# Swapping the first two weight loads of a decode kernel on one Trainium2 core

## The chip, the cores and the metric

The kernel runs on one core of one Trainium2 chip. The metric is device time in microseconds (us), the median of several executions; lower is better. In the profiles PE is the matrix engine (TensorE) and PEld its weight loads, DVE the vector, ACT the scalar and POOL the GpSimd engine; SP only issues transfers here. Profiles show one execution; their clock starts at the beginning of its span, and the span is about 1.3 us shorter than the device time.

## The reference, cut to what matters

One token passes through grouped-query attention with a long cache (part A) and through an MLP (part B), and the two results are added.

```python
x  = A_x                                    # [1, 1, 1024]
xn = layernorm(x)
# A: q = layernorm'd x @ wq; softmax over 4 KV heads x 65536 positions; @ wo
# B, called with x = xn:
h  = gelu(layernorm(x) @ w1)
g0 = pad(h[:, :, 0*c:1*c], one row in front)[:, :S]     # S = 1: only the padding is left
...                                                     # g1, g2, g3 likewise
hs = concat([g0, g1, g2, g3]) @ w2
x1 = x + hs
h2 = gelu(layernorm(x1) @ w3) @ w4
return x + A(xn) + (x1 + h2)
```

All data is bfloat16. What must be read is 169.87 MB: 134 MB of K and V, and the rest weights. wq and wo have 64 KB in each of 128 partitions (8.39 MB), w3 and w4 56 KB, w1 and w2 16 KB (2.1 MB).

## The kernel before

Three 64 KB slots per partition (`KV[:, 0..2]`) hold everything that is loaded. SP's queue carries all loads but one; x goes out on ACT's queue. These are the opening loads:

```python
_dma(q_act, chan("x"), lambda e: e.dma_start(out=x_bf, in_=...), writes=[b_x])   # 2 KB
kv_load(0, "s0", rows_src(A_wq, 0, 8), 8 * HQD)               # slot 0: wq, 64 KB a partition
kv_load(1, "w1", rows_src(B_w1, 0, 8), 8 * D, b_w1)           # slot 1, front: w1, 16 KB
_dma(q_sp, chan("w2"), ... KV[:, 1, 8 * D:16 * D] ...)        # slot 1, behind: w2, 16 KB
kv_load(2, "s2", rows_src(B_w3, 0, 8), 8 * F)                 # slot 2: w3, 56 KB
```

The compute of the opening follows in program order. Each `issue` sends a K or V block of 8.39 MB once its slot is free:

```python
cast x; constants; layer_norm(x)     # needs x
q projection                         # needs wq (slot 0) and the layer norm
issue(3)                             # first K block into slot 0
q to its layout; second layer norm
proj(w1); gelu; proj(w2)             # w2 times zeros
issue(4)                             # first V block into slot 1
third layer norm; proj(w3); gelu
issue(5)                             # second K block into slot 2
# then 8 blocks: transpose K, QK, exp, PV; each ends by issuing the next V and K
```

At the end of the program's construction, the first instruction of SP and of ACT, which must be a DMA, is moved in front of the barrier that opens the program:

```python
for eng in (nc.sync.engine, nc.scalar.engine):
    first = next(i for i in code[n_before:] if i.engine == eng)
    ...
    code.insert(code.index(heads[eng]), first)
```

Of the kernel before, what the change touches and what calls it, by code (L numbers as in the profile page):

```python
# [99 lines left out]
def _deps(q, reads, writes):  # L100
    evs = [e for b in reads for e in b.w.items()]
    for b in writes:
        evs += list(b.w.items()) + list(b.r.items())
    q.wait_all(evs, in_order=q.name == "pe")


def _done(ev, reads, writes, partial=False):
    for b in reads:
        b.add_read(ev)
    for b in writes:  # L110
        if partial:
            b.add_write(ev)
        else:
            b.set_write(ev)
# [24 lines left out]
def _dma(q, chan, fn, reads=(), writes=(), partial=False):  # L139
    _deps(q, reads, writes)  # L140
    chan.n += 1
    ev = q.dma(fn, chan.sem, 16 * chan.n)
    _done(ev, reads, writes, partial)
    return ev


def bass_parallel_sum__gqa_block_cached__mixer_s_mlp__decode_kernel(
# [16 lines left out]
    HQD = A_wq.shape[1]  # L164
# [14 lines left out]
    with ExitStack() as es:  # L179
# [8 lines left out]
        def sem(name):  # L188
            return E(nc.semaphore(name))
# [84 lines left out]
        def chan(name):  # L274
            if name not in chans:
                chans[name] = _DmaChan(sem("d_" + name))
            return chans[name]
# [11 lines left out]
        def kv_load(s, ch, src, n, bufs=None):  # L289
            _dma(q_sp, chan(ch), lambda e: e.dma_start(out=KV[:, s, 0:n], in_=src), writes=b_KV[s] if bufs is None else bufs)  # L290

        def rows_src(w, r0, nrow):
            return w.rearrange("(p r) n -> p (r n)", p=P)[:, r0 * w.shape[1]:(r0 + nrow) * w.shape[1]]

        _dma(q_act, chan("x"), lambda e: e.dma_start(out=x_bf, in_=A_x[0, 0, :].rearrange("(p j) -> p j", p=P)), writes=[b_x])
        kv_load(0, "s0", rows_src(A_wq, 0, 8), 8 * HQD)
        b_w1 = b_KV[1][0:2]
        b_w2 = b_KV[1][2:4]
        kv_load(1, "w1", rows_src(B_w1, 0, 8), 8 * D, b_w1)
        _dma(q_sp, chan("w2"), lambda e: e.dma_start(out=KV[:, 1, 8 * D:16 * D], in_=rows_src(B_w2, 0, 8)), writes=b_w2)  # L300
        kv_load(2, "s2", rows_src(B_w3, 0, 8), 8 * F)

# [427 lines left out]
```

## Time and profile before

| | before |
|---|---|
| time, median of the first 3 runs | 400.29 us |
| span of the profiled run | 399.3 us |
| load queue's packets, share of 16 DMA engines' span | 98.7% |
| DVE / PE busy | 55% / 45% |
| x lands, q projection starts | 22.4 us, 27.66 us |
| first K / first V / second K issued | 34.2 / 52.3 / 71.5 us |

From the page of the kernel before: the busy times (busy us, share of the span, instructions), the DMA queues (packets, MB, share), and the chain that ended last, by engine.

```profile
span 399.3 us, 3500 instructions
...
PE 177.8 (45%) x1539; PEld 61.1 (15%) x1539; DVE 221.3 (55%) x260; ACT 23.9 (6%) x50; POOL 7.7 (2%) x31
...
q1 hardware_dynamic: 3608, 169.87, 98.7%
...
q10 hardware_dynamic: 144, 0.00, 0.0%
...
DMA 58%; DVE 25%; PE 14%; issue 1%; ACT 1%; SPq 1%; POOL 0%
```

q1 is SP's queue with all the loads, and q10 is ACT's, with x alone. No compute engine is busy for more than 55% of the span, while q1's packets fill 98.7% of what 16 engines can do. The chain says 25% DVE, but that does not make DVE the limit: while DVE transposes, the load queue is still full.

The timeline of the kernel before (start us, duration, engine, line, operation, output and input, and in brackets the idle time before it and what ended it):

```profile
0.00 0.39 SPq L290 DMA_DIRECT2D KV<-in_A_wq_dram  x1
0.12 0.37 ACTq L295 DMA_DIRECT2D KV<-in_A_x_dram  x1
...
22.38 0.17 DVE L339 CAST KV<-KV 128x8 f32<-128x8 bf16 x1 [22.38 <-DMA KV<-in_A_x_dram]
...
27.66 6.49 PE L379 MATMUL S_ps<-KV 128*32 128x512 bf16 x64 [1.36 <-DVE KV L359]
28.07 0.16 PEld L379 LDWEIGHTS S_ps<-KV 128*32 128x32 bf16 x4 [0.27 <-issue]
28.49 0.16 PEld L379 LDWEIGHTS S_ps<-KV 128*32 128x32 bf16 x4 [0.27 <-issue]
...
34.21 0.33 SPq L290 DMA_DIRECT2D KV<-in_A_k_cache_dram  x1
...
101.21 0.33 SPq L290 DMA_DIRECT2D KV<-in_A_v_cache_dram  x1
```

x is 2 KB and lands after 22 us. All of the opening's compute stands behind it: the q projection waits for the layer norm (its releaser is DVE), not for wq.

The end of the chain of waits (start us, us, what):

```profile
363.85 32.93 DMA KV<-in_B_w_dram
396.78 0.04 issue
```

The run ends 2.5 us after the last piece of w4 lands.

### The profile page before, as it was taken

Reading aid. Unit: us, or ns where it says so; the run is one execution under the profiler, and the core shown is the slowest. Engines: PE = TensorE matmul, PEld = TensorE weight load, DVE = VectorE, ACT = ScalarE, POOL = GpSimd, SP = SyncE. Lnnn points to the kernel's source line nnn. Section 1 sums busy time; section 2 is a strip of 40 time slices with the busy share of each in tenths; the row PEclk is TensorE's granted clock in tenths of the full one; section 3 lists DMA queues with packets and bytes.
Section 4 is the critical chain, followed back from the end, with each engine's and each line's share of the span. In section 5 each row is a group of like instructions: output and inputs, shape, how many; then the busy total and the mean of one; then the engine's idle time right before and its main releaser. Section 6 shows DMA issues by size and latency. Waiting matters only on the chain.

```text
span 399.3 us, 3500 instructions
## 1 busy us (share of the span) xinstructions
PE 177.8 (45%) x1539; PEld 61.1 (15%) x1539; DVE 221.3 (55%) x260; ACT 23.9 (6%) x50; POOL 7.7 (2%) x31
## 2 busy tenths in 40 slices
PE   0035669147134713560358036413661462147394
PEld 0022435012001110110012001100120110012232
DVE  0024230995298539843984597269647952895201
ACT  1000000011001100110011002000100110011000
POOL 5000000000000000000000000000000000000000
PEclk9998656555755665585557555855565558555979
DMA  9999899999999999999999999999999999999995
GB/s 420 420 387 487 382 441 479 440 415 427 415 427 427 433 474 433 420 427 420 433 427 433 473 433 420 421 420 433 433 433 473 433 420 420 420 433 433 416 424 219
DMA packets 3759, 169.97 MB, mean 426 GB/s; under 512 B 548, under 2 KB 552, under 8 KB 808
## 3 DMA queue, kind: packets, MB, share of 16 engines
q1 hardware_dynamic: 3608, 169.87, 98.7%
q8 instruction: 5, 0.08, 0.1%
q10 hardware_dynamic: 144, 0.00, 0.0%
q14 instruction: 2, 0.02, 0.0%
HBM read 169.87 MB, written 0.00 MB: 425 GB/s over the span
## 4 chain that ended last, share of the span: by engine, by line
DMA 58%; DVE 25%; PE 14%; issue 1%; ACT 1%; SPq 1%; POOL 0%
DMA KV<-in_A_k_cache_dram 44%; DVE KV L460 17%; DMA KV<-in_B_w_dram 8%; DMA KV<-in_A_x_dram 6%; PE S_ps L411 3%; PE OT_ps L518 3%; DVE mrow L481 2%; PE M_ps L426 2%; PE S_ps L474 2%; PE S_ps L379 2%; ACT p_sb L496 1%; DVE Yall L395 1%; PE PT_ps L505 1%; DVE pT_f L509 1%; DVE pT_f L419 1%
## 5 line engine op out<-in xcount | busy, mean ns | idle before, releaser
L460 DVE STREAM_TRANSPOSE KV<-KV 128x4096 f32<-128x4096 f32 x32 | 140.3, 4421 | 42.2 <-DMA KV<-in_A_k_cache_dram 42.2
L474 PE MATMUL S_ps<-KV,Ycur 128*32 128x512 bf16 x512 | 60.7, 623 | 126.1 <-DVE KV L460 126.1
L518 PE MATMUL OT_ps<-KV,pT_f 128*32 128x512 bf16 x512 | 46.6, 504 | 1.2 <-DVE pT_f L509 1.2
L474 PEld LDWEIGHTS S_ps<-KV,Ycur 128*32 128x32 bf16 x512 | 14.3, 126 | 158.1 <-DVE KV L460 140.5
L496 ACT ACTIVATE p_sb<-S_ps,brun 128x1024 bf16<-128x1024 f32 x16 | 17.8, 1114 | 274.7 <-DVE brun L494 174.3
L509 DVE STREAM_TRANSPOSE pT_f<-PT_ps 128x512 f32<-128x512 f32 x32 | 22.4, 701 | 14.0 <-PE PT_ps L505 14.0
L481 DVE TENSOR_REDUCE mrow<-S_ps 128x1 f32<-128x1024 f32 x16 | 19.3, 1204 | 11.3 <-PE S_ps L474 11.3
L484 PE MATMUL M_ps<-Rm,Lmat 128*128 128x16 bf16 x16 | 3.1, 194 | 38.0 <-DVE Rm L482 38.0
L505 PE MATMUL PT_ps<-p_sb,permR 128*128 128x512 bf16 x32 | 18.3, 573 | 0.8
L529 DVE SCALAR_TENSOR_TENSOR O_acc<-O_acc,ff,OT_ps 128x512 f32<-128x512 f32 x12 | 9.0, 747 | 14.4 <-PE OT_ps L518 14.4
L518 PEld LDWEIGHTS OT_ps<-KV,pT_f 128*32 128x32 bf16 x512 | 12.9, 114 | 23.6 <-issue 15.5
L411 PE MATMUL S_ps<-KV 128*32 128x512 bf16 x88 | 12.5, 571 | 2.7 <-DVE KV L359 2.7
L339 DVE CAST KV<-KV 128x8 f32<-128x8 bf16 x1 | 0.2, 172 | 22.4 <-DMA KV<-in_A_x_dram 22.4
L578 PE MATMUL S_ps<-KV,o_bf 128*1 128x512 bf16 x64 | 9.7, 476 | 4.8 <-DMA KV<-in_A_wo_dram 4.8
L484 PEld LDWEIGHTS M_ps<-Rm,Lmat 128*128 128x128 bf16 x16 | 1.7, 104 | 49.3 <-DVE Rm L482 49.3
L426 PE MATMUL M_ps<-ident_f,pT_f 64*128 64x2 f32 (+2 forms) x32 | 7.9, 372 | 2.4 <-DVE pT_f L419 2.4
L582 DVE COPY pT_f<-S_ps 1x512 f32<-1x512 f32 x1 | 0.7, 679 | 14.4 <-PE S_ps L578 14.4
L426 PEld LDWEIGHTS M_ps<-ident_f,pT_f 64*128 64x128 f32 (+2 forms) x32 | 7.7, 326 | 4.7 <-DVE pT_f L419 3.4
L419 DVE COPY pT_f<-S_ps 64x512 f32<-64x512 f32 (+1 forms) x3 | 2.1, 685 | 11.3 <-PE S_ps L411 11.3
L505 PEld LDWEIGHTS PT_ps<-p_sb,permR 128*128 128x128 bf16 x32 | 3.3, 102 | 27.2 <-ACT p_sb L496 14.7
L364 PE MATMUL M_ps<-KV 8*128 8x8 bf16 x1 | 0.2, 182 | 16.2 <-DVE Dmat_f L363 16.2
L379 PE MATMUL S_ps<-KV 128*32 128x512 bf16 x64 | 6.5, 593 | 1.4 <-DVE KV L359 1.4
(88 smaller groups left out, 88.8 us busy)
## 6 DMA issues: line engine op xcount, KB each, us to landing
KV<-in_B_w_dram SPq DMA_DIRECT2D x1, 7168.0 KB, 48.4
KV<-in_B_w_dram SPq DMA_DIRECT2D x1, 4352.0 KB, 27.4
KV<-in_B_w_dram SPq DMA_DIRECT2D x2, 2048.0 KB, 28.4
KV<-in_B_w_dram SPq DMA_DIRECT2D x1, 1792.0 KB, 31.4
KV<-in_B_w_dram SPq DMA_DIRECT2D x1, 768.0 KB, 32.8
KV<-in_B_w_dram SPq DMA_DIRECT2D x1, 256.0 KB, 32.9
KV<-in_A_k_cache_dram SPq DMA_DIRECT2D x8, 46.5
KV<-in_A_v_cache_dram SPq DMA_DIRECT2D x8, 28.0
```

The source lines that it names most:

```text
L379: fns.append(lambda e, j=j, b=b, jj=jj: e.matmul(S_ps[32 * jj:32 * jj + 32, b, :], xn_bf[:, j:j + 1].broadcast_to([P, 32]), KV[:, 0, j * H ...
L411: fns.append(lambda e, j=j, k=k, mv=mv: e.matmul(S_ps[32 * (k % 4):32 * (k % 4) + 32, bank + k // 4, :], vec[:, j:j + 1].broadcast_to([P, ...
L426: fns.append(lambda e, b=b, nb=nb, c=c: e.matmul(M_ps[:, c0 + 16 * b + c:c0 + 16 * b + 4 * nb:4], pT_f[0:32 * nb, b, c:512:4], ident_f[0:3 ...
L460: _op(q_dve, lambda e: e.transpose(out=KV32[:, s, o:o + 4096], in_=KV32[:, s, o:o + 4096]), reads=[b_KV[s][sub]], writes=[b_KV[s][sub]], l ...
L474: fns.append(lambda e, we=we, cm=cm, mv=mv: e.matmul(S_ps[32 * cm:32 * cm + 32, n % 4, :], Ycur[:, we, :, :].rearrange("p a g -> p (a g)") ...
L481: _op(q_dve, lambda e: e.reduce_max(mrow[:, k:k + 1], S_ps[:, 2 * k:2 * k + 2, :].rearrange("p b c -> p (b c)"), axis=AX.X), reads=b_S[2 * ...
L496: _op(q_act, lambda e: e.activation(p_sb[:, :, :].rearrange("p b c -> p (b c)"), S_ps[:, 2 * k:2 * k + 2, :].rearrange("p b c -> p (b c)") ...
L505: _op(q_pe, lambda e: e.matmul(PT_ps[:, :], permR[:, :], p_sb[:, n % 2, :], start=True, stop=True), reads=[b_p[n % 2], b_const], writes=[b ...
L509: _op(q_dve, lambda e: e.transpose(out=pT_f[:, n % 2, :], in_=PT_ps[:, :]), reads=[b_PT], writes=[b_pT[n % 2]], loop=True)
L518: fns.append(lambda e, q=q, q4=q4: e.matmul(OT_ps[32 * q4:32 * q4 + 32, g % 2, :], pT_bf[:, n % 2, q, :, 1], KV[:, s, 8192 * sub + 512 * q ...
L529: _op(q_dve, lambda e: e.scalar_tensor_tensor(out=O_acc[:, 0:512], in0=O_acc[:, 0:512], scalar=ff[:, k:k + 1], in1=OT_ps[:, k, :], op0=ALU ...
L578: _grp(q_pe, [lambda e, j=j, jj=jj: e.matmul(S_ps[32 * jj:32 * jj + 1, 1, :], o_bf[:, j:j + 1], KV[:, 0, j * D + 512 * jj:j * D + 512 * (j ...
```

## The change

Its intent: x and w1 should be there early, so that the opening's compute starts sooner, since the first load in front of the barrier is then short.

```diff
         _dma(q_act, chan("x"), ...)
-        kv_load(0, "s0", rows_src(A_wq, 0, 8), 8 * HQD)
         b_w1 = b_KV[1][0:2]
         b_w2 = b_KV[1][2:4]
         kv_load(1, "w1", rows_src(B_w1, 0, 8), 8 * D, b_w1)
+        kv_load(0, "s0", rows_src(A_wq, 0, 8), 8 * HQD)
         _dma(q_sp, chan("w2"), ...)
```

The instructions of every engine other than SP are the same, in the same order.

## The prediction

> **What bounds the kernel now.** DMA. The page's queue table gives the load queue 98.7% of the 16 engines' span, 169.87 MB at 425 GB/s; DVE is busy 55%, PE 45%. In the chain of waits DMA has 58%, and the last w4 part lands at 396.8 us of 399.3. So the time is a start of about 1.3 us, 169.87 MB at the stream's rate, and a tail of 2.5 us. It changes only if the bytes, the rate, or the filling of the load queue change.
>
> **What the change does.** Bytes and number of loads stay. wq (8.39 MB) and w1 (2.1 MB) swap places; all others keep theirs. The load before the barrier goes out at 0.0 us, the next at 0.91; w1 alone is 5.0 us of stream at 420 GB/s (windows of the first 20 us), so the queue doesn't run dry.
>
> The visible effect is on x (2 KB, ACT's queue). Before, x was issued at 0.12 and landed at 22.4 us, together with wq. Its queue has 144 packets, nine for each of 16 engines. The Trainium skill, "DMA: Bandwidth & Descriptors", section "Queues, rings and completion order", says that each engine takes packets in turn from the queue rows that have work. Then x's eight small packets per engine alternate with eight 64 KB rows of wq, and x ends when wq does; the trace agrees (22.2 us to landing for both). With 16 KB rows of w1 in front, x ends with w1: about 5.0 + 2.2 = 7.2 us, or one or two wq rows (2.5 us each: 64 KB at a sixteenth of 420 GB/s) later: 7 to 12 us.
>
> The work hanging on x (cast, constants, first layer norm) took 22.4 to 27.6 us in the timeline, 5.3 us on the chain. It now runs under wq's load and ends by 13 to 17 us. But wq lands 5.0 us later, at about 27.2. So the q projection starts at about 27.3 instead of 27.66: 5.3 gained, 5.0 given back. An early w1 gains nothing: its projection stands behind the q projection and the second layer norm in program order.
>
> **On the critical path.** Almost nothing. About 0.4 us earlier from the q projection on: first K issue 33.9 (34.2), first V 52.0 (52.3), second K 71.2 (71.5). These are early already: w3 lands at 50.4 us, so the first K is issued 16 us before the queue would empty; estimated at 430 GB/s, the first K lands near 70 and the first V near 90, so the other two lead by about 18 us each. Later pairs are issued 7 us or more ahead of the stream's end (101.2 against 108.6). The queue stays full with or without the 0.4 us, and the last weight still lands at 396.8.
>
> **Predicted: 400.2 us, range 399.4 to 401.0.** Chances: faster by over 2% 0.01, within 2% 0.98, slower by over 2% 0.01.
>
> **What would show each step right or wrong.** Waits: DVE's 22.4 us wait for x falls to 7 to 12; the q projection's first matmul waits for wq's DMA. Timeline: q projection at 27.0 to 27.6, first K issue at 33.5 to 34.2. Queue table: share 98.5 to 99%, same bytes. Chain: its beginning changes from x to wq, its end doesn't; last weight at 396.8 within 0.6.
>
> **What would make it wrong.** If x landed behind wq after all (27 us), the q projection would start at 32.5 and the second V would be issued near 106, still 2 us ahead of the stream: the same time. A different rate of the stream, or a bubble between the first two loads, could cost or give about a microsecond; 2% would need 8 us of empty queue, for which I see no place.

## More of the kernel before

With one token (S = 1) all four shifted groups are zero, so `hs` is zero for finite weights. The kernel uses this in part: it multiplies w2 by a vector of zeros.

## The result, and the profile after

The kernel with the change took 400.73 us (median of 6 runs, 400.67 to 400.83) against 400.46 us before (6 runs, 400.26 to 400.55). The ratio is 1.0008, with a 95% interval of 0.9995 to 1.0021: the same. A ratio here compares the runs of both kernels by their means, so it is not quite the ratio of the medians. Executions over 1.5% slower than the fastest of the same kernel are left out of the means.

The same parts of the page after the change:

```profile
span 399.5 us, 3484 instructions
...
PE 170.0 (43%) x1523; PEld 61.4 (15%) x1539; DVE 221.4 (55%) x260; ACT 23.9 (6%) x50; POOL 7.6 (2%) x31
...
q1 hardware_dynamic: 3608, 169.87, 98.6%
...
DMA 60%; DVE 24%; PE 13%; issue 1%; ACT 1%; SPq 1%; POOL 0%
```

(The 16 matmuls fewer are records missing from the trace: the weight loads are all there, and the profile of the repeat below has all 1539 matmuls and 177.3 us.) The timeline after the change:

```profile
0.00 0.39 SPq L290 DMA_DIRECT2D KV<-in_B_w_dram  x1
0.12 0.37 ACTq L295 DMA_DIRECT2D KV<-in_A_x_dram  x1
...
0.92 0.33 SPq L290 DMA_DIRECT2D KV<-in_A_wq_dram  x1
...
10.36 0.17 DVE L339 CAST KV<-KV 128x8 f32<-128x8 bf16 x1 [10.36 <-DMA KV<-in_A_x_dram]
...
15.41 0.17 DVE L359 CAST KV<-KV 128x8 bf16<-128x8 f32 x1
27.41 5.04 PE L379 MATMUL S_ps<-KV 128*32 128x512 bf16 x64 [13.13 <-DMA KV<-in_A_wq_dram]
...
32.49 0.33 SPq L290 DMA_DIRECT2D KV<-in_A_k_cache_dram  x1
```

x lands 12.0 us sooner and the layer norm is done at 15.6 us, also 12.0 us sooner. Then PE idles until wq lands at 27.3 us. The projection starts 0.25 us sooner than before, and its releaser is now wq's DMA. The end of the chain of waits:

```profile
364.05 32.91 DMA KV<-in_B_w_dram
396.96 0.04 issue
```

The last piece of w4 lands at 396.96 us (396.78 before). The 1.7 us that the first K block was issued sooner (32.49 against 34.21) are gone by then. The chain shows where such a lead goes. The second K block, in the kernel before and then after the change:

```profile
71.52 37.07 DMA KV<-in_A_k_cache_dram
```

```profile
69.42 38.91 DMA KV<-in_A_k_cache_dram
```

It was issued 2.1 us sooner and landed only 0.26 us sooner (108.33 against 108.59); the rest it spent queued behind earlier loads. The chain counts a load from its issue, so it runs back through the opening (x's DMA before, wq's after), although the runs below show that the opening has slack.

**Why x landed when it did.** The trace has a record of every DMA packet: its queue, size, start and duration. The next table is worked out from these records. It gives the starts, in us after the first load packet, of x's 144 packets, sorted and cut into nine sets of 16 (one for each engine's share: eight of 16 bytes, then the one that signals the end).

```
set       before          after
1         3.07 -  3.87    1.99 - 2.68
2         5.49 -  6.29    2.77 - 3.29
3         7.91 -  8.71    3.38 - 3.99
4        10.33 - 11.13    4.04 - 4.60
...
8        20.01 - 20.27    6.05 - 6.55
9        20.28 - 20.82    8.26 - 8.97
```

Before, the first eight sets are 2.42 us apart, which is the duration of one 64 KB packet (median of all 2304 in the trace, 128 of them wq's: 2.421 us). After, the first seven are 0.58 to 0.78 us apart, about the duration of a 16 KB packet (median of the 256 of w1 and w2: 0.611 us); the last set falls behind a 64 KB packet of wq and takes 2.2 us more. This is what the Trainium skill, "DMA: Bandwidth & Descriptors", section "Queues, rings and completion order", states: an engine with work in two queue rows takes whole packets from them in turn. Here the load of tiny packets on the second queue moved at the pace of the other queue's packets, one a turn.

### The profile page after: what moved, and what is told of

It reads as the page before. It is cut to its first block, busy times and chain, and to the rows that moved or that the text cites. A ratio compares the mean times of both kernels' runs of the same rounds, so it can differ in the third digit from the quotient of the medians.

```text
span 399.5 us, 3484 instructions
## 1 busy us (share of the span) xinstructions
PE 170.0 (43%) x1523; PEld 61.4 (15%) x1539; DVE 221.4 (55%) x260; ACT 23.9 (6%) x50; POOL 7.6 (2%) x31
## 3 DMA queue, kind: packets, MB, share of 16 engines
q1 hardware_dynamic: 3608, 169.87, 98.6%
HBM read 169.87 MB, written 0.00 MB: 425 GB/s over the span
## 4 chain that ended last, share of the span: by engine, by line
DMA 60%; DVE 24%; PE 13%; issue 1%; ACT 1%; SPq 1%; POOL 0%
DMA KV<-in_A_k_cache_dram 45%; DVE KV L460 17%; DMA KV<-in_B_w_dram 8%; DMA KV<-in_A_wq_dram 7%; PE S_ps L411 3%; PE OT_ps L518 3%; DVE mrow L481 2%; PE M_ps L426 2%; PE S_ps L474 2%; PE S_ps L379 1%; ACT p_sb L496 1%; DVE Yall L395 1%; DVE pT_f L509 1%; DVE pT_f L419 1%; PE PT_ps L505 0%
## 5 line engine op out<-in xcount | busy, mean ns | idle before, releaser
L518 PE MATMUL OT_ps<-KV,pT_f 128*32 128x512 bf16 x512 | 47.6, 516 | 3.9 <-issue 3.1
L509 DVE STREAM_TRANSPOSE pT_f<-PT_ps 128x512 f32<-128x512 f32 x32 | 22.4, 701 | 14.0 <-PE PT_ps L505 14.0
L411 PE MATMUL S_ps<-KV 128*32 128x512 bf16 x88 | 12.2, 539 | 2.7 <-DVE KV L359 2.7
L379 PE MATMUL S_ps<-KV 128*32 128x512 bf16 x64 | 5.0, 484 | 13.1 <-DMA KV<-in_A_wq_dram 13.1
L505 PE MATMUL PT_ps<-p_sb,permR 128*128 128x512 bf16 x16 | 9.7, 608 | 0.8
```

Source lines behind the costliest of these rows:

```text
L379: fns.append(lambda e, j=j, b=b, jj=jj: e.matmul(S_ps[32 * jj:32 * jj + 32, b, :], xn_bf[:, j:j + 1].broadcast_to([P, 32]), KV[:, 0, j * H ...
L411: fns.append(lambda e, j=j, k=k, mv=mv: e.matmul(S_ps[32 * (k % 4):32 * (k % 4) + 32, bank + k // 4, :], vec[:, j:j + 1].broadcast_to([P, ...
L505: _op(q_pe, lambda e: e.matmul(PT_ps[:, :], permR[:, :], p_sb[:, n % 2, :], start=True, stop=True), reads=[b_p[n % 2], b_const], writes=[b ...
L509: _op(q_dve, lambda e: e.transpose(out=pT_f[:, n % 2, :], in_=PT_ps[:, :]), reads=[b_PT], writes=[b_pT[n % 2]], loop=True)
L518: fns.append(lambda e, q=q, q4=q4: e.matmul(OT_ps[32 * q4:32 * q4 + 32, g % 2, :], pT_bf[:, n % 2, q, :, 1], KV[:, s, 8192 * sub + 512 * q ...
```

## The experiments

All runs gave correct results. The kernel before ran beside them: 400.53 us (9 runs) beside the first four, 400.47 us (7 runs) beside the last two.

Two theories were set against each other. The *stream theory* is the prediction's: 169.87 MB must pass the 16 DMA engines, the load queue never runs empty, and the opening's compute only has to be early enough to keep it so. The *rival* says that the opening's chain is on the critical path, and that the change gained nothing only because wq, now 5 us later, gave back what x had gained.

### The change again

No edit to the changed kernel.

> The change again, with five rounds, to see whether its 0.2 to 0.3 us over the kernel before is real. The packet records of the two traces show the 16 DMA engines idle for 0.38 us on average in the first 20 us of the stream with the change and 0.18 us before. If that start is the cause: 0.1 to 0.3 us slower again (400.6 to 400.8 against 400.4), with the last weight again 0.2 us later. If it is chance: 0.0 within 0.1 us.

It took 400.6 us (5 runs) against 400.53: ratio 1.0003 (0.9989 to 1.0017). The engines' idle time in the first 20 us of the stream was 0.21 us this time (0.18 before, 0.38 in the first profile of the change), and the last weight landed at 396.77 us. So the difference of 0.27 us between the first two medians is not a property of the change that these runs can show.

### x in front of wq on the same queue

```diff
-        _dma(q_act, chan("x"), ...)
+        _dma(q_sp, chan("x"), ...)
         kv_load(0, "s0", rows_src(A_wq, 0, 8), 8 * HQD)
 ...
-        for eng in (nc.sync.engine, nc.scalar.engine):
+        for eng in (nc.sync.engine, nc.sync.engine):
```

> x and then wq on the same queue, both in front of the opening barrier. x lands at 2 to 4 us, wq at 22.5 to 23; the first layer norm runs under wq, and nothing is given back by a later wq. Theory (the DMA stream bounds the kernel, the opening only moves slack): the q projection starts near 22.8 us, 5 us sooner than in both kernels, and the time stays 400.0 to 401.0. Rival (the opening chain is on the critical path, and the change gained nothing only because the later wq gave the 5 us back): 395 to 396 us.

It took 400.85 us (5 runs), ratio 1.0009 (0.9995 to 1.0022): the same. Its timeline:

```profile
1.65 1.15 DVE L339 CAST KV<-KV 128x8 f32<-128x8 bf16 x1 [1.65 <-DMA KV<-in_A_x_dram]
22.54 5.38 PE L379 MATMUL S_ps<-KV 128*32 128x512 bf16 x64 [11.39 <-DMA KV<-in_A_wq_dram]
...
27.96 0.33 SPq L290 DMA_DIRECT2D KV<-in_A_k_cache_dram  x1
46.48 0.33 SPq L290 DMA_DIRECT2D KV<-in_A_v_cache_dram  x1
64.85 0.33 SPq L290 DMA_DIRECT2D KV<-in_A_k_cache_dram  x1
99.58 0.33 SPq L290 DMA_DIRECT2D KV<-in_A_v_cache_dram  x1
```

With nothing queued ahead of it x landed 1.65 us into the span, and the q projection started 5.1 us sooner than before. The first K was issued 6.3 us sooner, the second K 6.7 us sooner, and the second V only 1.6 us sooner (99.58 against 101.21). The time did not move. x landed a little before the expected 2 to 4 us. The rival wanted 395 to 396 us, and falls.

### x behind w2, and x behind w3

```diff
-        _dma(q_act, chan("x"), ...)                 # removed here
 ...
         _dma(q_sp, chan("w2"), ...)
+        _dma(q_sp, chan("x"), ...)                  # x_behind_w2
         kv_load(2, "s2", rows_src(B_w3, 0, 8), 8 * F)
+        _dma(q_sp, chan("x"), ...)                  # or x_behind_w3
 ...
-        for eng in (nc.sync.engine, nc.scalar.engine):
+        for eng in (nc.sync.engine,):
```

> x on the load queue behind w2, so it lands with w2 at about 32.3 us and the q projection starts about 9.9 us later than before, at 37.6. Theory with margins read from the trace: first K, first V and second K are still issued before the queue runs empty; the next V/K pair is issued at about 111 instead of 101.2, against K landing at 108.6, so the queue runs empty there once: 3 to 6 us slower (403.5 to 406.5). If the first K's lead of 16 us were the smallest margin, as the prediction's other figures could be read: no change (400.5). Rival (opening on the critical path): 10 us slower (410).

> x on the load queue behind w3, so it lands at about 50.5 us and the q projection starts 28 us later, at 55.7. Theory: the first K is issued at 62 with the queue empty since about 49 (14 us lost), and the second V/K pair again after the queue has run empty (another 7 to 9 us): 21 to 23 us slower in all, 420 to 424. Rival (opening on the critical path): the whole 28 us, 428.

x_behind_w2 took 405.46 us (4 runs, 404.86 to 406.94), ratio 1.013 (1.011 to 1.015). The q projection started at 37.13 us, 9.5 us later than before; the time grew by 4.9 us. These are its q projection and SP issues in the timeline, and then its windows (from:to, length, busy time of PE, PEld, DVE, ACT and POOL with counts, granted clock (the share of its full clock that PE was given), share of the DMA engines, GB/s):

```profile
37.13 5.84 PE L379 MATMUL S_ps<-KV 128*32 128x512 bf16 x64 [1.36 <-DVE KV L359]
...
80.14 0.33 SPq L290 DMA_DIRECT2D KV<-in_A_k_cache_dram  x1
109.59 0.33 SPq L290 DMA_DIRECT2D KV<-in_A_v_cache_dram  x1
109.96 0.87 SPq L290 DMA_DIRECT2D KV<-in_A_k_cache_dram  x1
```

```profile
100.00:105.00 5.00, 3.90 (x35) 0.85 (x23) 2.41 (x6) 1.29 (x3) 0.00 (x0) 0.50 1.00 433
105.00:110.00 5.00, 4.36 (x50) 1.28 (x50) 2.41 (x5) 0.00 (x1) 0.00 (x0) 0.85 0.04 16
110.00:115.00 5.00, 0.03 (x4) 0.03 (x8) 5.00 (x4) 0.00 (x0) 0.00 (x0) 0.83 1.11 419
```

(The windows count a packet where it starts, so one stretch can exceed 1.) The same windows of the kernel before:

```profile
100.00:105.00 5.00, 1.05 (x16) 0.34 (x16) 0.94 (x3) 0.00 (x0) 0.00 (x0) 1.00 1.02 436
105.00:110.00 5.00, 0.00 (x0) 0.00 (x0) 1.39 (x1) 0.00 (x0) 0.00 (x0) 0.52 0.94 406
110.00:115.00 5.00, 1.89 (x16) 0.45 (x16) 5.00 (x2) 0.00 (x0) 0.00 (x0) 0.50 0.97 419
```

The queue ran empty exactly once, between 105 and 110 us: the second V and third K came at 109.6 us, when the second K's packets had all gone. By the packet records the engines idled 4.41 us there (0.06 before). (The records do not name the engine; idle is counted from how many of 16 packets are in flight.) The pair was issued 8.4 us later than before (109.59 against 101.21), so about 4 us of the delay were absorbed.

x_behind_w3 took 422.46 us in a single look (state unknown), 21.9 us more than before. From its timeline:

```profile
54.20 5.92 PE L379 MATMUL S_ps<-KV 128*32 128x512 bf16 x64 [1.36 <-DVE KV L359]
...
60.17 0.33 SPq L290 DMA_DIRECT2D KV<-in_A_k_cache_dram  x1
...
126.80 0.33 SPq L290 DMA_DIRECT2D KV<-in_A_v_cache_dram  x1
```

The q projection began at 54.20 us, 26.5 us later. The packet records show 13.4 us of idle engines before the first K block, 7.6 us before the second V block, and 1.9 us elsewhere (2.1 in all in the kernel before). A chain on the critical path would have cost the whole 26.5 us.

### Without the compute on w1 and w2; without the loads too

```diff
-        layer_norm(xn, b_xn, xn2, xn2_bf, b_xn2, 204)
 ...
-        proj(1, 0, D, xn2_bf, 2, b_w1 + [b_xn2], 256)
-        gelu(M_ps[:, 256:256 + KT_D], KT_D, h1g_bf, b_M, b_h1)
-        proj(1, 8 * D, D, g_bf, 3, b_w2 + [b_const], 272)
-        ... the two adds of its zero result
         issue(4)
-        layer_norm(x1, b_x1, xn3, xn3_bf, b_xn3, 208)
+        layer_norm(xn, b_xn, xn3, xn3_bf, b_xn3, 208)
```

no_loads has this edit and also leaves out the two DMAs of w1 and w2.

> The kernel before, all loads kept, but without what computes on w1 and w2: second layer norm, two projections, gelu, two adds. With one token the four shifted groups are all zero, so w2 is multiplied by zeros and the result stays exact. This takes about 16 us of work out of the opening chain (39.6 to 55.3 us). Theory (bytes bound it): 400.0 to 401.0. Rival (work of the opening counts): up to 15 us faster, 385.

> As no_proj, and w1 and w2 are not loaded either: 4.19 MB less of 169.87. Theory: faster by the stream's time for these bytes, 256 packets of 16 KB at 0.611 us on 16 engines, 9.8 us: 390.2 to 391.2, unless the queue runs empty in the shorter opening (w3 now lands near 40.5 us, first K issued near 34). Rival (work of the opening counts): the same as no_proj, or much less than it by only what the first loads hold up.

no_proj took 400.4 us (4 runs), ratio 0.9996 (0.9979 to 1.0013): the same, although the second K block was issued at 60.75 us instead of 71.52:

```profile
60.75 0.33 SPq L290 DMA_DIRECT2D KV<-in_A_k_cache_dram  x1
```

no_loads took 390.62 us (4 runs), ratio 0.9755 (0.9738 to 0.9771): faster. Its page:

```profile
span 389.2 us, 3357 instructions
...
PE 156.9 (40%) x1471; PEld 53.7 (14%) x1487; DVE 217.4 (56%) x242; ACT 23.7 (6%) x49; POOL 7.1 (2%) x30
...
q1 hardware_dynamic: 3320, 165.68, 98.7%
```

The queue's share is 98.7% as before, with 4.19 MB less to move.

### All runs by the packet records

This table is worked out from the packet records of each profile, for the load queue's packets of 2 KB and more. "Packets" is the sum of their durations, divided by 16 engines; "idle" is the engines' mean idle time between the first and the last of them.

```
run            time us     packets us   idle us   packets + idle
before         400.46      393.81        2.08      395.9
the change     400.73      393.81        2.23      396.0
r_after        400.60      393.94        1.90      395.8
x_first        400.85      393.78        1.86      395.6
x_behind_w2    405.46      394.54        6.38      400.9
x_behind_w3    422.46      395.05       22.81      417.9
no_proj        400.40      393.62        1.94      395.6
no_loads       390.62      384.02        1.76      385.8
```

(r_after is the change again.) The time is packets plus idle plus 4.5 to 5.2 us of start, end and what lies outside the span, in every run. The sum counts overlap at the seams, so it is a little above the stream's length. No run moved the time without moving one of the two columns, and the change moved neither. The sum by itself is bookkeeping; the test is that each edit moved the column that its expectation named, by about the size it named. In the kernel before, 1.54 of the 2.08 us of idle lie in the last stretch, where the engines finish w4 and have no more work.

## Why the prediction was right

The predicted 400.2 us (399.4 to 401.0) met 400.73 us, and the class "within 2%" was right. Point by point:

- **The bound.** "It changes only if the bytes, the rate, or the filling of the load queue change" was shown by the runs above. no_loads changed the bytes (9.8 us of packets, 9.85 us of time), the two late-x kernels changed the filling, and three kernels that changed neither kept the time.
- **x lands at 7 to 12 us.** It landed at 10.4. The turn-taking of the queues is visible packet by packet.
- **5.3 us gained, 5.0 given back.** The q projection was to start at 27.3 us and started at 27.41, released by wq as predicted.
- **First K at 33.9 us (33.5 to 34.2).** It was issued at 32.49: this step missed, and so did the first V (52.0 predicted, 51.22 measured) and the second K (71.2 and 69.42) behind it. The prediction kept the projection's duration, 6.49 us, and it took 5.04. The groups of four matmuls start 0.42 to 0.43 us apart at first in both kernels. The trace's first clock record, of a full clock, starts at 33.49 us before and at 30.30 us after; there the pace changes, in both, to a group every 0.22 us. The Trainium skill, "TensorE: Matmul & The Clock Gate", section "Wait — 56ns, not 53.3ns?", gives 426.7 ns for 512 columns on a cold array (at half clock), and this trace agrees. Why the clock rose 2.9 us into the projection in one kernel and 5.8 us in the other is not shown here; that page says, in the section "What's actually happening", that the window in which activity is measured runs freely, which would explain it, but no run here tests it. The error had no weight, because this step has slack: x_first issued the first K 6.3 us sooner and the time stayed.
- **The leads.** "The other two lead by about 18 us each" holds for the first blocks, but the smallest margin in the opening is that of the second V and third K. The prediction gave it as "7 us or more", from issue (101.2) to landing (108.6). x_behind_w2 puts it at about 4 us. Two things eat into the lead. A block lands with the slowest engine: by the packet records of the kernel before, twelve of the 16 engines had ended the second K block 1.8 us before the last one did. And new packets start some time after their issue: 0.9 us in x_behind_w2 (issue at 109.59, first packets from 110.5). The lead must be counted from an engine's last packet to its next one, not from issue to landing.
- **If x landed late, "still 2 us ahead of the stream".** This sentence about an alternative (the pair issued near 106) is too bold by the same error. x_behind_w2, with the pair at 109.6, lost 4.9 us; at 106 about 1 us would have been lost, by an estimate from its 4 us of margin (101.2 + 4 = 105.2).

## What to carry to other kernels

In this kernel the load queue is full from start to end, and the order of the first loads and the compute that they release were worth nothing, as long as each next load was issued before the queue ran empty. In such a case ask how much earlier than necessary the next load is issued, and count it from the last packet sent to the first packet of the new load. Then look for bytes to drop: here the weights multiplied by a structural zero were 2.5% of the traffic and 2.5% of the time. no_loads is the fastest kernel (390.62 us); it is exact only for one token and finite w1 and w2, and would be wrong for a longer sequence.

The tiny load on a second queue beside a bulk load waited one of the bulk load's packets for each of its own here; putting it in front on the same queue (landed at 1.65 us instead of 22.4) cost nothing that these runs can show (ratio 1.0009) and is worth trying where the chain behind it does count.

## What the Trainium skill lacked or had wrong

- "DMA: Bandwidth & Descriptors", section "Queues, rings and completion order", says that engines switch queues at packet boundaries, and calls 9 to 17 descriptors a packet typical; its section "SWDGE vs HWDGE vs iDMA" prefers packets of at most 4,096 bytes where GpSimd builds them; neither says how long a turn can be. Here a packet of a contiguous row is the whole row, up to 65,536 bytes, and a turn lasts 2.42 us. So a 2 KB load took 22.2 us from issue to landing beside a 64 KB-row load, 10.2 us beside a 16 KB-row load followed by a 64 KB-row one, and 1.6 us in front of the bulk load on its queue.
- No page says that a profile's clock row has no information before the first clock record. The windows show a granted clock of 1.00 from 28 to 33 us in the kernel before, while groups of four 512-column matmuls start 0.42 to 0.43 us apart; behind the first record, at 33.49 us, they start 0.22 us apart.
